# Products with v for two units at a time, a planner with other TensorE times, and the gather's place before the weight splits

## The chip, the cores and the metric

The kernel runs on one core of a Trainium2 chip. The metric is the time of one execution on the device in microseconds (us). A core has five engines with an instruction queue each: TensorE (PE, with PEld for its weight loads), VectorE (DVE), ScalarE (ACT), GpSimd (POOL) and SyncE (SP, which here only issues DMAs). An engine takes its instructions in the order in which they stand in its queue; engines wait for each other through semaphores.

## The reference, cut to what matters

```python
def _attn_ref(q, k, v):                      # 4 x 8 x 576 x 64
    scores = scale * np.matmul(q, k.transpose(0, 1, 3, 2))
    kth = np.partition(scores, -32, axis=-1)[..., -32:-31]
    scores = np.where(scores >= kth, scores, -1000000000.0)
    attn = np.exp(scores - np.max(scores, axis=-1, keepdims=True))
    attn = attn / (np.sum(attn, axis=-1, keepdims=True) + 1e-09)
    return np.matmul(attn, v)
def _moe_ref(x, w_in, w_out):                # 2304 x 512 x 2048
    h = x @ w_in
    return (h * np.cos(h)) @ w_out
def _moe2_ref(x, w_gate, w1, w2):            # 8 experts, 288 tokens each
    order = np.argsort(-(x @ w_gate).flatten())
    for idx in order:                        # a token goes to its best expert that has room
        ...
    for e in range(8):
        out[assigned == e] = np.maximum(x[assigned == e] @ w1[e], 0.0) @ w2[e]
    return out
```

## The kernel before, in words

**Attention.** The rows of the score matrices are handled in 72 units: 8 for the last 64 rows of the heads (called remainder units), then 64 that each hold 128 rows of two heads. For a unit, PE makes the scores (`qk`, L592), ACT takes them out of PSUM (L599), DVE finds the 32nd largest of each row with rounds of MAX8 and MATCH_REPLACE (L633 to L649), ACT and POOL mask and exponentiate (L664 to L676), DVE zeroes what lies below the threshold and sums (`zero`, L681). Then PE transposes the weights (L745 to L749), ACT copies them out (`eT`, L755), and PE multiplies them with v (`pv`, L770 and L772; L777 and L779 in remainder units). Beside that runs the divisor: POOL makes it from the sums (`div`, L797), DVE inverts it (`recip`, L794), POOL widens it (`wide`, L800), PE transposes it (`Rm`, L805), ACT copies it out (`R`, L809), and DVE scales the product into `xr` (`scale`, L823; L820 in remainder units). Before, each of these steps is made once per unit.

**MLP.** Every 8 units fill a block of 256 tokens (9 blocks). A block's `xr` is split into a high and a low part (L873, L878), multiplied with w_in in three products (`mm1`, L328, 12 matmuls a step), passed through h*cos(h) (L340 to L369 on ACT, DVE and POOL), split again (L893, L897) and multiplied with w_out (`mm2`, L912). Its rows of y go to DRAM, and its gate logits are made on PE (L935 to L965).

**Tail.** When the attention is over, constants are set on POOL and DVE (`late_consts`, L1068 to L1102, the last of them `wog_`, the gate weights that the logits of the last block need). The last block's MLP, its logits (`lg4`, L396) and the routing in rounds (`cmp` L1194, `cnt` L1200) follow, beside the last block's y. The routing ends in `idx` (L1378). POOL then gathers the first expert's rows with indirect DMAs (`xg`, L1417), while DVE makes the low parts of the first experts' weights (`w2l`, task `wlo`, L1048). Then the loop over experts runs: gather (L1563), transposes (L1627, L1631), first product (L1584), `hl` (L1588), second product (L1599). It splits weights `LA` chunks ahead.

**What sets the order.** Class `Plan` is a list scheduler that runs when the program is built. Each step is a task with an engine, a duration in ns, the tasks that it follows, the buffers that it takes and gives, and a rank to which a number from the tables `OFFSETS` and `TAIL_OFFSETS` is added. At each step the planner starts the task that can start first; among those of one engine that are within a small margin the lower rank wins. It adds `SW` = 95 ns when PE changes its tiling (table `MODE`: 64x128 for `qk`, 128x64 for `pv`, 128x128 for most others). The result is only an order of instructions on each engine: on the chip an instruction waits for the semaphores of its own operands and buffers and for nothing else that the planner thought of.

Of the kernel before, what the change touches and what calls it, by code (L numbers as in the profile page):

```python
# [9 lines left out]
F32 = mybir.dt.float32  # L10
# [13 lines left out]
NCAND = 8  # L24


def f32(ap):
# [11 lines left out]
    "L": -3.75, "Re": -2.25, "Re_0": -5.5, "Re_r": 6, "Rm": 4, "Rm_0": -2.25, "Rm_r": 5.5, "bias": 7, "bias_0":  # L39
    -4.75, "bias_r": 6.5, "big": 5.75, "big_0": 5.75, "big_r": -0.5, "count": 3.25, "div": -7.75, "div_0": 1.75,  # L40
    "div_r": 5, "eT": -2.25, "eT_0": -8.25, "eT_r": 2.75, "evac": -4.25, "evac_0": -7.25, "evac_r": -3.5, "exp":
# [3 lines left out]
    "less_0": -1.25, "low_in": -5.75, "low_out": -3, "mag_in": 2.5, "mag_out": 8, "mask": 2.75, "mask_0": 3,  # L45
    "mask_r": -3, "mm1": 3.75, "mm1_0": 5.5, "mm2": 9.25, "mm2_0": 10, "near": 0, "near_0": -4.75, "other": 2,
    "other_0": -1.5, "other_r": 4, "pl": 2.25, "pv": 0.75, "pv_0": -9.5, "pv_r": -4.25, "qk": -0.5, "qk_0": -4.5,
    "qk_r": 4.25, "recip": -1.25, "recip_0": 6, "recip_r": -2.5, "scale": 3.25, "scale_0": -8.75, "scale_r": 4.25,
    "sg_in": -2.75, "sg_out": 2.25, "shift_in": -10, "shift_out": 3, "sine": -4, "sine_0": 5, "small": 5, "small_0":
    -4.25, "small_r": -7.25, "strike": 5.75, "strike_0": 8, "strike_r": 10, "top": 8, "top_0": 10, "top_r": -4.75,  # L50
    "total": -8.75, "tr": 3.25, "tr_0": -4, "tr_r": 7.75, "v": 3.75, "wH_in": 3, "wH_out": -1.25, "wL_in": -10,
    "wL_out": -6.5, "w_in": 7, "w_out": 10, "whole": -0.5, "wide": 8, "wide_0": 7.25, "wl": 4.25, "wl_0": -5, "wp":
    1, "wraw_in": 3.25, "wraw_out": 8.75, "wse": 2, "wst_out": -4.75, "wt": -9.75, "wte": -5, "xH": -9.75, "xL":
    -0.5, "yT": 2.5, "yd": -1.75, "ys": 2.5, "yt": 4.5, "zero": -7.5, "zero_0": 4, "zero_r": -8.25
# [5 lines left out]
    "L": 7, "all": 2.25, "am": -7, "amd": 5.25, "any": 4.5, "asg": -8.75, "before": 1.25, "cmp": 1.5, "cnt": -2.75,  # L60
    "columns": 5.75, "excess": -8, "first": -7, "gH": -8.25, "gH_e": 2.25, "gL": 3, "gL_e": -8.5, "gate": 7.25,
    "go": 1.25, "here": 2.5, "higher": 4.75, "hot": -0.5, "hs": -7.25, "in_column": -3.25, "in_row": -2.5, "less":
    1.75, "lg": 3.5, "lg4": 3.25, "listed": -3.25, "lt": 9.25, "mm1": -5, "mmT": -1.75, "near": 0, "next": 0,
    "numbers": 9, "places": 0.25, "prop": 4.5, "rise": 7.75, "rows": 2.25, "shares": 4.25, "sine": 2.75, "slots": 3,
    "square": 3.5, "start": 2, "sums": -4.25, "tokens": -1, "verdict": 2, "wh": 3.25, "wl": 4, "wlo": 6.25, "woL":
    4.25, "woL_e": 3.5, "woL_f": 4.5, "wrong": -3.25, "xg": 7.5, "y": 1, "y_e": 0.75, "y_f": -4.75, "yd": 3.5,
    "yd_e": -3, "yd_f": 3, "ys": 7, "ys_e": 9.75, "ys_f": 0.5, "z": 3.25, "zd": -2.75
# [3 lines left out]
class Plan:  # L71
# [6 lines left out]
    SW = 95  # L78
    HOLD_PE = 0
# [9 lines left out]
    def add(self, key, eng, ns, fn, after=(), take=(), give=(), rank=0, table=None, lat=0):  # L89
# [4 lines left out]
        port = eng == "POOL" and key[0] != "xg" or eng == "DVE" and key[0] in self.PORT and not (key[0] == "less" and key[1] in LESS_DVE)  # L94
# [40 lines left out]
    def run(self):  # L135
# [29 lines left out]
        while len(order) < len(ts):  # L165
# [27 lines left out]
            if t["mode"]:  # L193
                f = work(s, t["ns"] + (self.SW if t["mode"] != mode else 0))
                mode = t["mode"]
            else:
                f = s + t["ns"] + (self.TABLE if sw else 0)
# [23 lines left out]
def fused_kernel(ctx: ExitStack, tc: tile.TileContext, qT: bass.AP, kT: bass.AP, qR: bass.AP, kR: bass.AP, v9: bass.AP,  # L221
# [62 lines left out]
    def everything(fold, ctx):  # L284
# [30 lines left out]
        def hidden1(plan, T, psum, mp, m, need, rank, stay=None):  # L315
# [103 lines left out]
        def phase1():  # L419
# [13 lines left out]
            for vt in vts:  # L433
# [6 lines left out]
                kp=3, qp=2, vt=2, x=3, m8=3, nm=2, w=2, tb=2, eT=4, rs=2, ri=2, rw=1, R=2, xr=1, xHL=1,  # L440
                hs=3, kr=1, gH=2, gL=2, wl=4, ys=2, yT=1)
# [134 lines left out]
            def qk(j):  # L576
# [27 lines left out]
                for c in range(2):  # L604
                    last = [("qk", j, 0)] if c else [("qk", j - 1, 1)] if j else []
                    add(("qk", j, c), "PE", 1160 if rem else 590, prod(c), need + last, [("pS", j, c)], give, rank=j - 1)
# [3 lines left out]
            def topk(j):  # L610
# [60 lines left out]

                def expo(h):
                    if ("rs", j) not in T:
                        new(ap, "rs", j, [128, 2])
                    sums = T["rs", j][:, h:h + 1]
                    A.activation(w_(h) if mode == "T" else x_(h), x_(h), AF.Exp, bias=T["nm", j][:, h:h + 1], scale=0.125,  # L676
                                 accum_out=None if mode == "T" else sums)

                def zero(h):
                    sums = T["rs", j][:, h:h + 1]  # L680
# [34 lines left out]
                for h in range(2):  # L715
# [5 lines left out]
                    rs = [("rs", j)] if h == 0 else []  # L721
# [6 lines left out]

            def pv(j):

                rem, b, hp, t = unit(j)
                u = key(j, 0)

                parts = [(h, n) for h in range(2) for n in range(5)] if rem else [(None, n) for n in range(9)]
                chunks = [parts[a:a + 3] for a in range(0, len(parts), 3)]
# [22 lines left out]
                def prod():  # L758
                    o_ = new(psum, "pT", ("pv", j), [128, 128])
                    if rem:  # L760
                        o_ = o_.rearrange("p (h q) -> p h q", h=2)
                    for c, i in [(c, i) for c in range(len(chunks)) for i in range(len(chunks[c]))]:
                        h, n = chunks[c][i]
                        eT = T["eT", (j, c)][:, i, :]
                        for a in range(2):
                            p = slice(a * 64, (a + 1) * 64)
                            if h is None:
                                o = o_[p]
                                if n == 8:
                                    PE.matmul(o, T["vt", u][:, 8 + a], eT, start=False, stop=True)  # L770
                                elif n % 2 == a:
                                    PE.matmul(o, T["vt", u][:, n, :], eT, start=(n < 2), stop=False)  # L772
                            else:
                                o = o_[p, h]
                                v = T["vt", u + h]
                                if n < 4:
# [933 lines left out]
```

## Time and profile before

| | us |
|---|---|
| median of 3 runs (1118.85, 1121.01, 1121.40) | 1121.01 |
| the profiled execution, time | 1117.51 |
| the profiled execution, span from first to last instruction | 1115.5 |
| PE busy | 1031.5 (92%) |
| DVE busy | 915.9 (82%) |
| ACT busy | 799.6 (72%) |
| POOL busy | 546.9 (49%) |
| mean granted TensorE clock | 0.966 |

An engine's busy share is an average over stages: the attention with the MLP of the earlier blocks, the tail, and the experts. The stages are read apart below. The granted clock is a share of TensorE's full speed of 2.4 GHz; 0.50 is its lower level, 1.2 GHz, and numbers between are mixtures of the two in one stretch.

### The profile page before, as it was taken

To read this page: it belongs to the slowest core of one execution; us is meant where nothing else is said; L and a number is where in the kernel's file an instruction comes from. 1 tells how busy PE (TensorE), PEld (TensorE's weight loads), DVE (VectorE), ACT (ScalarE), POOL (GpSimd) and SP (SyncE) were. 2 spreads that over 40 slices of the span, in tenths; PEclk is the share of its full clock that TensorE was granted. 3 is DMA by queue.
4 is the path that set the end of the run, shared out by engine and by line. 5 is a ranking of instruction groups with operands and counts; after the bars stand their busy time and mean duration, and the time that the engine had idled before them with its cause. 6 is when DMAs were issued, how large, how long until landed. Compare 5 with 4: busy or idle time off the path is not lost. (4 is left out here: it accounts for less than half of the span.)

```text
span 1115.5 us, 22521 instructions
## 1 busy us (share of the span) xinstructions
PE 1031.5 (92%) x7972; PEld 866.0 (78%) x7972; DVE 915.9 (82%) x2510; ACT 799.6 (72%) x1463; POOL 546.9 (49%) x710
## 2 busy tenths in 40 slices
PE   4666998899999999999999999998998899999995
PEld 1444876677888878878888888887866799999995
DVE  6999999999999999999999999995497455555530
ACT  4887889798988988888888988987420455555531
POOL 5985777766655654654755655655002202222211
PEclk9987898999999999999999999999999799999998
DMA  7474533434423323333233233212258746666601
GB/s 234 153 223 155 169 110 106 158 112 127 123 90 102 94 84 109 99 85 110 82 94 117 85 93 108 86 50 67 78 168 286 249 152 194 194 195 195 195 26 39
DMA packets 88441, 144.97 MB, mean 130 GB/s; under 512 B 15744, under 2 KB 36736, under 8 KB 88320
## 3 DMA queue, kind: packets, MB, share of 16 engines
q1 hardware_dynamic: 85248, 134.01, 38.6%
q0 software_dynamic: 3072, 9.44, 3.0%
q8 instruction: 65, 1.06, 0.4%
q14 instruction: 56, 0.46, 0.1%
HBM read 129.52 MB, written 13.89 MB: 129 GB/s over the span
## 5 line engine op out<-in xcount | busy, mean ns | idle before, releaser
L642 DVE MAX8 m<-w 128x8 f32<-128x288 f32 (+1 forms) x576 | 239.1, 449 | 1.5
L646 DVE MATCH_REPLACE8 w<-m,w 128x288 f32<-128x288 f32 x432 | 189.0, 442 | 0.0
L328 PE MATMUL pH<-xH,wiH 128*128 128x256 f32 x576 | 174.8, 304 | 3.8 <-DVE kr L359 3.3
L328 PE MATMUL pH<-xL,wiH 128*128 128x256 f32 x576 | 164.1, 285 | 0.0
L328 PE MATMUL pH<-xH,wiL 128*128 128x256 f32 x576 | 164.0, 285 | 0.0
L592 PE MATMUL two<-kp,qp 64*128 64x288 f32 (+1 forms) x640 | 129.0, 491 | 28.8 <-ACT x L599 18.8
L670 POOL TENSOR_TENSOR x<-x,w 128x576 f32<-128x576 f32 x76 | 109.5, 1455 | 29.2 <-ACT w L664 29.0
L755 ACT ACTIVATE eT<-pT 128x384 f32<-128x384 f32 x224 | 105.7, 479 | 24.2 <-PE pT L745 18.6
L328 PEld LDWEIGHTS pH<-xH,wiH 128*128 128x128 f32 x576 | 111.3, 193 | 8.6 <-DVE kr L359 4.4
L1048 DVE TENSOR_TENSOR w2l<-w2raw,w2h 128x1024 fp32r<-128x1024 f32 x64 | 77.9, 1224 | 41.2 <-ACT w2h L1045 39.2
L328 PEld LDWEIGHTS pH<-xL,wiH 128*128 128x128 f32 x576 | 111.3, 193 | 0.3
L328 PEld LDWEIGHTS pH<-xH,wiL 128*128 128x128 f32 x576 | 111.0, 193 | 0.0
L1616 POOL DMA_INDIRECT out<-ot,idx x24 | 22.3, 930 | 178.7 <-ACT ot L1614 178.3
L599 ACT ACTIVATE x<-two 128x576 f32<-128x576 f32 x144 | 93.5, 649 | 19.4 <-PE two L592 10.8
L592 PEld LDWEIGHTS two<-kp,qp 64*128 64x128 f32 (+1 forms) x640 | 49.6, 188 | 68.5 <-ACT x L599 28.9
L745 PE MATMUL pT<-ident,x 128*128 128x128 f32 x576 | 97.7, 279 | 3.3 <-DVE x L681 1.2
L369 POOL TENSOR_TENSOR hs<-hs,kr 128x512 f32<-128x512 f32 x56 | 75.6, 1368 | 42.9 <-ACT kr L364 41.8
L912 PE MATMUL pY<-wo,gH 128*128 128x512 f32 x224 | 96.4, 430 | 0.0
L745 PEld LDWEIGHTS pT<-ident,x 128*128 128x128 f32 x576 | 67.8, 142 | 30.0 <-issue 14.0
L897 POOL TENSOR_TENSOR gL<-hs,gH 128x512 fp32r<-128x512 f32 x56 | 75.8, 1353 | 30.8 <-ACT gH L893 24.7
L912 PE MATMUL pY<-wl,gH 128*128 128x512 f32 x224 | 88.2, 394 | 0.0
L912 PE MATMUL pY<-wo,gL 128*128 128x512 f32 x224 | 87.9, 392 | 0.0
(228 smaller groups left out, 2939.8 us busy)
## 6 DMA issues: line engine op xcount, KB each, us to landing
w2raw<-w SPq DMA_DIRECT2D x64, 512.0 KB, 4.7
wl<-wl_d SPq DMA_DIRECT2D x112, 256.0 KB, 2.7
vt<-v SPq DMA_DIRECT2D x48, 256.0 KB, 2.7
woL<-wl_d SPq DMA_DIRECT2D x46, 256.0 KB, 3.8
kp<-kT SPq DMA_DIRECT2D x32, 288.0 KB, 3.1
room<-w_in SPq DMA_DIRECT2D x16, 512.0 KB, 4.3
room<-w_out SPq DMA_DIRECT2D x16, 512.0 KB, 3.5
kp<-kR SPq DMA_DIRECT2D x16, 288.0 KB, 4.5
```

The costliest lines, as they stand in the source:

```text
L328: PE.matmul(ph, lw[:, c, fs], rx[:, c, :], start=(k == 0), stop=(k == 3 * KD - 1))
L369: (G if m - 1 + i in GATE_POOL else V).tensor_tensor(h, h, T["kr", m // 2][:, 2 * i:2 * i + 2], op=OP.mult)
L592: PE.matmul(o, lhsT, T["kp", us[h]][p, s], start=True, stop=True)
L599: A.activation(T["x", j][:, :, c * hS:(c + 1) * hS], T["pS", (j, c)][:, :, :hS], AF.Copy)
L642: V.max(m8_(h, 8 * k), w_(h, 0, hS + (8 if k == TOPK // 8 - 1 else 0)) if fold else w_(h))
L646: V.match_replace(w, m8_(h, 8 * k), x_(h) if k == 0 and not fold else w, -BIG)
L670: G.tensor_tensor(x_(h), x_(h), w_(h), op=OP.subtract if mode == "S" else OP.add)
L745: PE.transpose(pT[:, i, :], e[:, c0:c0 + 128], ident)
L755: A.activation(new(ap, "eT", (j, c), [128, 3, 128])[:, :n], T["pT", ("e", j, c)][:, :n], AF.Copy)
L897: (G if m in GL_POOL else V).tensor_tensor(gL, T["hs", m], f32(T["gH", m]), op=OP.subtract)
L912: PE.matmul(T["pY", blk][t], T[g, m][:, i, ts], w, start=(f == 0 and n == 0), stop=(f == KF - 1 and n == 2))
L1048: eng.tensor_tensor(WS[n][1], WR.pop(n), f32(WS[n][0]), op=OP.subtract)
```

## The change

Four things change. The steps from `div` to `scale` are made once for two units (a group) in every unit that is not a remainder; the number of matmuls is the same, the other instructions become half as many and twice as wide. The planner gets other durations for PE's tasks, a price for each change of tiling from a table, a margin in rank (`HOLD_PE` = 8) against changing it, and new tables of offsets, so that the order changes on every engine. Buffers change: `eT` 4 to 7, `R` 2 to 1, `ys` 2 to 1 in the attention, `kr` 1 to 2 in the tail, and some tiles of the routing share memory. The low parts of the weights are planned behind the third gather, and `LA` goes from 9 to 6. The numbers of the two tables tell nothing and are left out.

```diff
-    "L": -3.75, "Re": -2.25, "Re_0": -5.5, "Re_r": 6, "Rm": 4, "Rm_0": -2.25, "Rm_r": 5.5, "bias": 7, "bias_0":
+    "L": 4.5, "Re": 0.75, "Re_0": 10, "Re_r": -4.25, "Rm": 0.25, "Rm_0": -4.5, "Rm_r": 4.75, "bias": 4.5, "bias_0":
...
-    SW = 95
-    HOLD_PE = 0
+    SWITCH = {("128x128", "64x128"): 92, ("64x128", "128x128"): 229, ("64x128", "128x64"): 228, ("128x128", "128x64"): 131,
+              ("128x64", "128x128"): 414, ("128x64", "64x128"): 414}
+    def switch(self, old, to):
+        return 0 if to in (None, old) else self.SWITCH.get((old, to), 150)
+    HOLD_PE = 8
...
-        port = eng == "POOL" and key[0] != "xg" or eng == "DVE" and key[0] in self.PORT and not (key[0] == "less" and key[1] in LESS_DVE)
+        port = eng == "POOL" or eng == "DVE" and key[0] in self.PORT and not (key[0] == "less" and key[1] in LESS_DVE)
...
-                add(("mm1", m, i), "PE", 1440, one(i), after, [] if i else [("pH", m)], [("xHL", m // BW)], rank=rank)
+                add(("mm1", m, i), "PE", 1508, one(i), after, [] if i else [("pH", m)], [("xHL", m // BW)], rank=rank)
...
-                kp=3, qp=2, vt=2, x=3, m8=3, nm=2, w=2, tb=2, eT=4, rs=2, ri=2, rw=1, R=2, xr=1, xHL=1,
-                hs=3, kr=1, gH=2, gL=2, wl=4, ys=2, yT=1)
+                kp=3, qp=2, vt=2, x=3, m8=3, nm=2, w=2, tb=2, eT=7, rs=2, ri=2, rw=1, R=1, xr=1, xHL=1,
+                hs=3, kr=1, gH=2, gL=2, wl=4, ys=1, yT=1)
...
+            def group(j):
+                return j if j < NWR else NWR + (j - NWR) // 2
+            def members(g):
+                return [g] if g < NWR else [2 * g - NWR, 2 * g - NWR + 1]
+            def together(g):
+                js = members(g)
...
+                    o_ = new(psum, "pT", ("pv", g), [128, 128 * len(js)])
...
-                add(("pv", j), "PE", 1700 if rem else 985, prod, need + [("Rm", j)] + ([("pv", j - 1)] if j else []), [("pT", "pv", j)],
+                add(("pv", g), "PE", 1700 if rem else 1658, prod, eTs + [("v", u)] + ([("v", u + 1)] if rem else []) + [("Rm", g)] + ([("pv", g - 1)] if g else []),
...
-                        V.tensor_mul(xr[:, hp, t % 2 * 128:(t % 2 + 1) * 128], o_, R[:, 0])
+                        V.tensor_mul(xr[:, hp], o_, R.rearrange("p i q -> p (i q)"))
...
-        NCH, LA, NRAW = 12, 9, 4
+        NCH, LA, NRAW = 12, 6, 4
...
-        plan.bufs.update(pH=2, pY=2, pt=1, pc=1, pp=1, xHL=1, kr=1, gH=7, gL=7, woL=6, ys=1, lg=1, w2raw=NRAW)
+        plan.bufs.update(pH=2, pY=2, pt=1, pc=1, pp=1, xHL=1, kr=2, gH=7, gL=7, woL=6, ys=1, lg=1, w2raw=NRAW)
...
-                add(("wlo", n), "DVE", 1200, lambda: w_low(n, V), [("wh", n), ("tokens", )], give=[("w2raw", n)], rank=rank)
+                add(("wlo", n), "DVE", 1200, lambda: w_low(n, V), [("wh", n), ("xg", 2) if fold else ("tokens", )], give=[("w2raw", n)], rank=rank)
```

The line numbers after the change are higher by 5 (MLP) to 37 (the end of the attention's units), and by 35 in the tail.

**TensorE in the steady part of the attention.** Before, one unit's product with v (L772 and L770, 20 matmuls in 10 rows of order) stands between two stretches of MLP or scores:

```order
L328 MATMUL pH<-xL,wiH 128x256
L328 MATMUL pH<-xH,wiL 128x256
L592 MATMUL two<-kp,qp 128x288 x2
L772 MATMUL pT<-eT,vt_123 64x128 x8
L770 MATMUL pT<-eT,vt_123 64x128 x2
L745 MATMUL pT<-ident,x 128x128 x3
L912 MATMUL pY<-wo,gH 128x512
```

Now the products of two units stand together (L810 and L808), and the stretches between them are twice as far apart:

```order
L333 MATMUL pH<-xL,wiH 128x256
L333 MATMUL pH<-xH,wiL 128x256
L597 MATMUL two<-kp,qp 128x288 x2
L810 MATMUL pT<-eT,vt_122 64x128 x8
L808 MATMUL pT<-eT,vt_122 64x128 x2
L810 MATMUL pT<-eT,vt_122 64x128 x8
L808 MATMUL pT<-eT,vt_122 64x128 x2
L597 MATMUL two<-kp,qp 128x288 x2
```

What moved: every second entry into the tiling of the products with v, and every second way out of it, is gone.

**TensorE at the end of the attention.** Before, the last products with v are followed by 96 rows of the last block's `mm1` (L328), and only then by the logits that need `wog_` (L396):

```order
L745 MATMUL pT<-ident,x 128x128 x9
L805 MATMUL pT<-ident,rw 128x128
L772 MATMUL pT<-eT,vt_123 64x128 x8
L770 MATMUL pT<-eT,vt_123 64x128 x2
L328 MATMUL pH<-xH,wiH 128x256
L328 MATMUL pH<-xL,wiH 128x256
...
L328 MATMUL pH<-xH,wiL 128x256
L396 MATMUL pp<-room,wog__10014 32x256 x16
L328 MATMUL pH<-xH,wiH 128x256
```

Now the rows of y and of the gate (L980, L992) and the 16 matmuls of `lg4` that need `wog_` (L401) stand ahead of every `mm1` of the last block (L333):

```order
L810 MATMUL pT<-eT,vt_123 64x128 x8
L808 MATMUL pT<-eT,vt_123 64x128 x2
L810 MATMUL pT<-eT,vt_123 64x128 x8
L808 MATMUL pT<-eT,vt_123 64x128 x2
L980 MATMUL pT<-ident,ys 128x128 x4
L992 MATMUL pT<-wg,yT 128x8 x4
L401 MATMUL pp<-room,wog__9662 32x256 x16
L333 MATMUL pH<-xH,wiH 128x256
L333 MATMUL pH<-xL,wiH 128x256
```

What moved: `lg4` of the block before the last went from behind 96 rows of `mm1` to ahead of all of them.

**DVE at the gather and the first expert.** Before, the low parts of the weights (L1048) stand right behind `idx` (L1378), and three more of them stand between the parts of the first expert's rows (`xl`, L1567) and `hl` (L1588):

```order
L1378 TENSOR_SCALAR idx<-idf 96x24
L1048 TENSOR_TENSOR w2l<-w2raw,w2h 128x1024 x6
L1567 TENSOR_TENSOR xl<-po_11137,xh 128x288
L1567 TENSOR_TENSOR xl<-po_11138,xh 128x288
L1567 TENSOR_TENSOR xl<-po_11139,xh 128x288
L1567 TENSOR_TENSOR xl<-po_11140,xh 128x288
L1048 TENSOR_TENSOR w2l<-w2raw,w2h 128x1024 x3
L1588 SCALAR_TENSOR_TENSOR hl<-ph,hh 128x288
```

Now two small operations of the routing (`fl`, `fa`) stand between `idx` (L1413) and the low parts (L1082), and none stands ahead of the first `hl` (L1623):

```order
L1413 TENSOR_SCALAR idx<-idf 96x24
L1321 TENSOR_REDUCE fl<-c_9674 128x1
L1325 TENSOR_TENSOR fa<-fc,fl 128x1
L1082 TENSOR_TENSOR w2l<-w2raw,w2h 128x1024 x6
L1602 TENSOR_TENSOR xl<-po_10782,xh 128x288
L1602 TENSOR_TENSOR xl<-po_10783,xh 128x288
L1602 TENSOR_TENSOR xl<-po_10784,xh 128x288
L1602 TENSOR_TENSOR xl<-po_10785,xh 128x288
L1623 SCALAR_TENSOR_TENSOR hl<-ph,hh 128x288
L1082 TENSOR_TENSOR w2l<-w2raw,w2h 128x1024
```

What moved: three of the nine low parts that stood ahead of the first `hl` went behind it; the first six still follow `idx`, with no instruction between that waits for the gather.

## Rows read from the trace of the kernel before

**Rows 1.** Stages (us, busy us of PE, PEld, DVE, ACT, POOL, granted clock, DMA share).
```profile
50.00:100.00 50.00, 34.34 (x334) 21.52 (x332) 48.59 (x138) 39.82 (x81) 36.73 (x39) 0.80 0.65 201
...
400.00:450.00 50.00, 50.00 (x403) 40.31 (x398) 47.98 (x148) 41.72 (x76) 24.10 (x36) 1.00 0.34 100
...
900.00:950.00 50.00, 50.00 (x391) 50.00 (x390) 28.43 (x42) 26.58 (x45) 7.70 (x11) 1.00 0.57 176
```

**Rows 2.** Waits of PE, 0 to 300 (total, times, longest); two MAX8 in DVE's timeline.
```profile
PE two L592 <- ACT x L599: 18.8, 18, 3.3
...
407.16 0.82 DVE L642 MAX8 m<-w 128x8 f32<-128x288 f32 x2
```

**Rows 3.** Waits of PE and then of DVE, 300 to 765.
```profile
PE pT L805 <- POOL rw L800: 0.2, 1, 0.2
...
DVE xr L823 <- PE pT L770: 5.8, 18, 0.7
```

**Rows 4.** One product with v on PE (timeline); PE instructions (x) in two windows.
```profile
407.50 1.09 PE L772 MATMUL pT<-eT,vt 128*64 128x128 f32 x16
...
408.74 0.50 PE L912 MATMUL pY<-wo,gH 128*128 128x512 f32 x1
...
407.70:408.14 0.44, 0.44 (x12) 0.44 (x10) 0.44 (x3) 0.43 (x2) 0.44 (x1) 1.00 0.57 74
407.70:408.58 0.88, 0.88 (x20) 0.87 (x16) 0.88 (x5) 0.87 (x2) 0.88 (x2) 1.00 0.71 177
```

**Rows 5.** Groups by line on DVE and ACT (busy us, mean ns, idle before).
```profile
L823 DVE TENSOR_TENSOR xr<-pT,R 128x128 f32<-128x128 f32 x64 | 18.2, 284 | 10.9 <-PE pT L770 9.9 <-ACT x L676 0.5
...
L794 DVE RECIPROCAL ri<-ri 128x2 f32<-128x2 f32 x72 | 11.0, 152 | 4.3 <-POOL ri L797 3.8
...
L809 ACT ACTIVATE R<-pT 128x128 f32<-128x128 f32 x64 | 17.8, 278 | 0.3 <-PE pT L805 0.2
...
L809 ACT ACTIVATE R<-pT 128x256 f32<-128x256 f32 x8 | 3.0, 375 | 2.3 <-PE pT L805 2.3
```

**Rows 6.** End of the attention phase: DVE, PE, and a window of clock.
```profile
776.32 0.56 DVE L1102 COPY wog__10014<-wog 128x128 f32<-128x128 f32 x1
776.80 1.28 DVE L359 TENSOR_TENSOR kr<-pH,kr 128x512 f32<-128x512 f32 x2
...
768.57 0.28 PE L328 MATMUL pH<-xH,wiL 128*128 128x256 f32 x1
...
772.53 0.28 PE L328 MATMUL pH<-xH,wiL 128*128 128x256 f32 x1
...
777.50:780.00 2.50, 2.47 (x11) 2.47 (x12) 1.28 (x2) 1.15 (x1) 2.50 (x3) 0.50 0.64 221
```

**Rows 7.** The gather: timeline of DVE, POOL and PE.
```profile
854.98 0.17 DVE L1378 TENSOR_SCALAR idx<-idf 96x24 int32<-96x24 f32 x1
855.07 4.62 DVE L1048 TENSOR_TENSOR w2l<-w2raw,w2h 128x1024 fp32r<-128x1024 f32 x4
...
855.50 5.21 POOL L1417 DMA_INDIRECT xg<-y_d,idx  x1 [44.99 <-DVE idx L1378]
...
862.24 0.92 POOL L1417 DMA_INDIRECT xg<-y_d,idx  x1 [0.30 <-issue]
...
867.61 5.98 PE L1627 MATMUL po<-ident,xg 96*128 96x96 f32 x24 [6.43 <-DMA xg<-y_d,idx]
```

**Rows 8.** First expert: DVE, PE, and two windows after it.
```profile
878.42 3.50 DVE L1048 TENSOR_TENSOR w2l<-w2raw,w2h 128x1024 fp32r<-128x1024 f32 x3 [0.49 <-issue]
881.83 0.45 DVE L1588 SCALAR_TENSOR_TENSOR hl<-ph,hh 128x288 fp32r<-128x288 f32 x1
...
882.33 0.40 PE L1584 MATMUL ph<-xh,w2h 128*128 128x288 f32 x1 [2.17 <-DVE hl L1588]
...
882.50:885.00 2.50, 2.50 (x14) 2.50 (x15) 1.42 (x3) 1.11 (x2) 0.00 (x0) 0.63 1.02 296
885.00:887.50 2.50, 2.50 (x15) 2.50 (x15) 2.16 (x3) 1.42 (x2) 0.00 (x0) 0.68 1.07 374
```

More of the change, by code (lines that the diff above doesn't have):

```diff
@@ L47 @@
[L47 to L51, printed above, removed]
@@ new lines @@
+    -6.75, "low_out": -10, "mag_in": 7, "mag_out": -2.75, "mask": 0.25, "mask_0": -5, "mask_r": 0, "mm1": 3.5,
+    "mm1_0": 4.75, "mm2": 8.5, "mm2_0": 3.5, "near": 7.75, "near_0": 8.5, "other": 3.25, "other_0": 8.75, "other_r":
+    -0.25, "pl": 10, "pv": 2.5, "pv_0": -5.25, "pv_r": 5.25, "qk": -8.75, "qk_0": -2.25, "qk_r": -0.75, "recip":
+    -8.75, "recip_0": -7, "recip_r": -8, "scale": -4.75, "scale_0": -6.5, "scale_r": 0.5, "sg_in": -2.25, "sg_out":
+    -7.25, "shift_in": -3.5, "shift_out": -7.75, "sine": 10, "sine_0": 10, "small": -9.25, "small_0": -4.75,
@@ L59 @@
 TAIL_OFFSETS = {
[L60 to L67, printed above, removed]
+    "L": -5.75, "all": -5, "am": 8.75, "amd": -3.5, "any": 6.5, "asg": -3.25, "before": -2.5, "cmp": 8, "cnt": 7,
+    "columns": 7.25, "excess": 5, "first": 5, "gH": 7.25, "gH_e": 8, "gL": -2.5, "gL_e": -1.25, "gate": 1.25, "go":
+    -2.25, "here": 5.5, "higher": 5, "hot": -5.25, "hs": -4.5, "in_column": -6.75, "in_row": 7, "less": 4.5, "lg":
+    -10, "lg4": 5.75, "listed": 4, "lt": -7.75, "mm1": 7.25, "mmT": 3.5, "near": 4.25, "next": 0, "numbers": 0.5,
+    "places": 5.5, "prop": -5.75, "rise": 9, "rows": -9.5, "shares": -7.5, "sine": 2.25, "slots": -3.75, "square":
+    1, "start": -5.25, "sums": 7, "tokens": -2.75, "verdict": 5.25, "wh": -0.75, "wl": 2.5, "wlo": -3, "woL": -4.25,
+    "woL_e": -4.25, "woL_f": 1.25, "wrong": 2.25, "xg": 2.75, "y": -8.75, "y_e": 1.25, "y_f": -1.25, "yd": -5.5,
+    "yd_e": -7.75, "yd_f": -1.5, "ys": 6, "ys_e": -2, "ys_f": 4.75, "z": -3.5, "zd": 4.5
 }
@@ L193, in run @@
             if t["mode"]:
-                f = work(s, t["ns"] + (self.SW if t["mode"] != mode else 0))
+                f = work(s, t["ns"] + self.switch(mode, t["mode"]))
                 mode = t["mode"]
@@ L727, in topk, with parts_of @@
                         add(("zero", i), "DVE", 740, lambda h=h: zero(h), [("exp", i)], give=w + m8, rank=j + 1)
+            def parts_of(j):
+                parts = [(h, n) for h in range(2) for n in range(5)] if j < NWR else [(None, n) for n in range(9)]
+                return [parts[a:a + 3] for a in range(0, len(parts), 3)]
             def pv(j):
[L731 to L735, printed above, removed]
+                rem = j < NWR
+                chunks = parts_of(j)
                 rank = j + 1
@@ L756, in out_ @@
                     return fn
[L758 to L776, printed above, removed]
-                                    PE.matmul(o, v[:, 2 * n + a, :], eT[:, p], start=(n == 0), stop=False)
-                                else:
-                                    PE.matmul(o, v[:, 8 + a, :], eT[:, p], start=False, stop=True)
                 for c in range(len(chunks)):
@@ L783, in pv @@
                     last = [("tr", j, c - 1)] if c else [k for k in [("tr", j - 1, 3), ("tr", j - 1, 2)] if k in plan.tasks][:1]
-                    if j and c == (0 if rem else 1):
-                        last.append(("pv", j - 1))
-                    add(("tr", j, c), "PE", 15 + 108 * n, turn(c), [("zero" if MODES[j] == "T" else "exp", 2 * j + h) for h in range(2)] + last, [("pT", "e", j, c)],
+                    if j and c == (0 if rem else 1) and (("pv", group(j) - 1) in plan.tasks):
+                        last.append(("pv", group(j) - 1))
@@ L881, in block @@
                 for c in range(HP):
-                    need = [("scale", w) for w in last if unit(w)[2] // 2 == c // 2] if blk == 0 else [("scale", last[2 * c + i]) for i in range(2)]
+                    need = [("scale", w) for w in last if unit(w)[2] // 2 == c // 2] if blk == 0 else [("scale", group(last[2 * c]))]
                     add(("xH", blk, c), *(("DVE", 340) if (blk, c) == LAST else ("ACT", 310)), x_high(c), need + ([("xH", blk, c - 1)] if c else []),
@@ L1166, in all_max @@
             return r
-        av = small("av", [128, NTI, E])
-        vv = small("vv", [128, NTI, E])
+        avv = small("avv", [128, 2, NTI, E])
+        av, vv = avv[:, 0], avv[:, 1]
         best = small("best", [128, NTI])
```

123 lines of the change are left out of this document (78 added, 45 removed), and 7 rows, old and new, of the table OFFSETS.

## The prediction

> **What bounds the kernel now.** I read the busy times by stage first, then the waits of the engine that is not full, then the timeline at the places where the order changes. Early in the attention DVE is the full engine: between 50 and 100 us it is busy for 48.59 of 50 us and PE for 34.34 [rows 1], and PE's largest wait up to 300 us is for score tiles that ACT has to empty, 18.8 us in 18 pieces [rows 2]; ACT in turn waits for units that DVE has not finished. From some 300 us to the end of the attention at about 768 us PE is full (50.00 of 50 us at 400) with DVE close behind at 47.98 [rows 1]. In that stretch PE's waits are of 0.2 us, while DVE waits 5.8 us for products with v [rows 3]. So DVE's work counts for the first 300 us and PE's own work for the next 470. Then come the tail, with waits on every engine, and the experts, where PE is full at clock 1.00 and DVE at 28.43 of 50 us [rows 1].
>
> **The two-unit products, on PE.** One product with v holds PE from 407.50 to 408.74 us, 1.24 us for 20 matmuls [rows 4]. Inside it, widening a window by 0.44 us adds 8 matmuls (12 to 20), so one takes 0.055 us and twenty 1.10 [rows 4]. The other 0.14 us is the way into and out of the tiling. The two-unit form makes this once for two units. By the order, 48 of the 64 units are scaled in the stretch where PE is full, so 24 visits go there: 24 x 0.14 = −3.4 us. In the DVE-bound stretch a shorter PE gives nothing. The bounds are nothing (the entry is hidden by the weight load) and 24 x 0.28 = −6.7 (both neighbours of a visit also become cheaper); I take the value of the row. The planner's new table instead prices the way out at 0.414 us, which would be 24 x 0.414 = −9.9; a visit that costs 1.24 in all with 1.10 of matmuls leaves no room for that. The Trainium skill ("TensorEngine Tiling (Array Packing)", Key Properties) says that a change of tiling mode drains TensorE; the rows agree and give the drain its size, 0.14 us, and by the planner's reading of that rule the term would be the −9.9.
>
> At the end of the attention the last pair is one visit instead of a visit that was partly made earlier: its second 1.10 us now lies behind the last unit's transposes, which is the path. That is +1.1.
>
> **The two-unit divisor and scaling, on DVE.** A scaling takes 284 ns and an inversion 152 [rows 5]. What doubling the width costs DVE is not in the trace; ACT's copy of the same size goes from 278 to 375 ns when its width doubles, 97 ns for 128 more columns [rows 5]. I take a wide scaling at 0.42 us, some 0.15 less than two, and an inversion saved at 0.10, since neighbours overlap: 0.25 us for a pair. Bounds are 0 and 0.44 (284 + 152, the whole second pair of operations). Ahead of the scaling of the 16th unit that is 8 x 0.25 = −2.0 (0 to −3.5). By the order four operations of the top-32 that stood ahead of this point now stand behind it, and one `kr` more stands ahead: net −1.5 at 0.5 us each, an estimate between a MAX8 (two in 0.82 us [rows 2]) and a `kr` (two in 1.28 [rows 6]). Together −3.5 for the DVE-bound stretch. In the PE-bound stretch the 24 x 0.25 = 6 us saved on DVE are worth nothing; they lengthen DVE's waits for products. POOL and ACT, at 24.10 and 41.72 of 50 us in that stretch [rows 1], are not what PE waits for, so half as many `wide` and `R` go at nothing. `R` and `ys` with one buffer each hold the next `Rm` or y row until DVE or the DMA is done; with PE's waits in this stretch at 0.2 us [rows 3] I take nothing, at most +2.
>
> Sum to the end of the attention: −3.4 + 1.1 − 3.5 = **−5.8** (−10 to +2).
>
> **The end of the attention.** DVE sets the tail's constants and ends them with `wog_`, which runs from 776.32 to 776.88; from 776.80 it makes `kr` of the last block [rows 6]. Before, PE uses this time: 33 `mm1` matmuls take 3.96 us (768.57 to 772.53), 0.12 each, and 48 of them, as many as PSUM holds, end at 774. Now `lg4` waits for `wog_` at the head of PE's queue, 8.3 us after the 768.57, and all `mm1` of the last block queue behind it. The DVE instructions of this chain and their order are the same, so the chain is as late as before. So 48 x 0.12 = 5.8 us of products that were hidden come behind it, and the first `kr` on DVE has to wait for the first 24 of them. What the last block loses is 5.8, plus some of the low clock: already after a pause of 3 us PE ran at 0.50 between 777.5 and 780 [rows 6], and now it pauses for 8. Against it stand two `kr` buffers in place of one, which free DVE of waits for ACT's sine. Sum **+6.2** (+4 to +8). The rounds behind it keep their form: I find +1.4 and −1.3 from single small operations that change places, and take nothing.
>
> **The gather.** Before, DVE's four low parts run from 855.07 to 859.69 without a gap and the first gather instruction on POOL takes 5.21 us from 855.50; the third, alone, takes 0.92 [rows 7]. PE then waits 6.43 us for the gathered rows, until 867.61 [rows 7]. This is the loss that the new order of `wlo` aims at: 4.3 us. But the planner's dependency puts no wait on DVE. The low parts follow `idx` after two small operations, about 0.3 us later, still before POOL's 855.50, so that four of them again run ahead of and through the gather: **0**, against −4.3 if the gather gets in first. The Trainium skill ("SBUF — State Buffer", SBUF: two separate sides) has a shared port that a GpSimd operation or a DVE operation with two SBUF inputs holds for a whole instruction. By the letter of it POOL would come in after the first low part; the row shows it kept out through four.
>
> **The first expert.** Three low parts (3.50 us from 878.42) stand ahead of `hl` at 881.83, PE idles 2.17 us for it, and then runs 5 us at clock 0.63 and 0.68 [rows 8]. At full clock these 5 us would be 3.3. Without the three low parts `hl` comes at once: −2.2, and −1.7 for the clock if the pause was what lowered it. I take **−3.6** (−1 to −4). The three parts are made a few us later in a stage where DVE has over 20 of 50 us free [rows 1], so their move costs nothing unless the first chunk that they make is used within those us.
>
> **Sum.** −5.8 + 6.2 + 0 − 3.6 = −3.2. The profiled execution took 1117.51 us, which is 3.5 under the median of 1121.01, so against the median the time is 1121.01 − 3.2 = **1117.8 us**, against the profiled execution 1114.3.
>
> **Rivals.** *First block late.* By the order, seven MAX8, six MATCH_REPLACE and one conversion of weights (L481) more stand on DVE ahead of the scaling of the last remainder unit, which is most of one more unit's top-32. At 0.41 us a piece (two MAX8 in 0.82 [rows 2]) that is 14 x 0.41 = 5.7 us more DVE work ahead of the first block's `mm1`, in a stretch where DVE has 1.4 us of slack in 50 [rows 1]. If PE, which fills up only after 300 us, does not catch this up, the −3.5 becomes +2.2; with the +6.2 at the end of the attention at +8 and the −3.6 at −2, the sum is −3.4 + 1.1 + 2.2 + 8 − 2 = +5.9, 1126.9. It decides if block 1's first product starts later than now. Against it: that extra unit is work done ahead, so DVE has less behind it. *The gather gets ahead.* If the two small operations take longer than POOL's 0.35 us from `idx` to gather, POOL is first and the gather takes 0.92: −3.2 − 4.3 = −7.5, 1113.5. *DVE was the bound throughout.* PE in its full stretch may only look full because its operations stretch while waiting; then the attention ends earlier by all 32 x 0.25 = 8 us of DVE and 1.5 of moved operations: −9.5 + 1.1 + 6.2 − 3.6 = −5.8, 1115.2; DVE's 5.8 us of waits for PE speak against it [rows 3]. *The switch is dear.* With 0.414 for each the −3.4 is −9.9 and the sum −9.7, 1111.3; the 1.24 us visit speaks against it.
>
> **How the numbers follow.** About 0.3% or 3.4 us is what a measurement of this kernel can tell from no change. My forecast, −3.2, lies on that edge: chance 0.55, somewhat under half of it faster by more than that, the rest the same. First block late, 0.18, nearly all slower. Gather ahead 0.12, DVE the bound 0.08, the dear switch 0.07, all faster. So faster 0.21 + 0.27 = 0.48, same 0.34, slower 0.18. The range leaves out the ends of the dear switch and half of the late block: 1109 to 1125.
>
> **What would show it.** Right: visits of 2.3 us for two units; 8 us of PE idle ahead of `lg4` at the end of the attention, and the attention itself 6 us shorter; the first gather instruction again at 4 to 5 us; no wait of 2 us for the first `hl`. Wrong: an attention that ends later than 768 us, a tail from there to `idx` that is not longer than now, or a gather of 0.9 us.

## The result, and the profile after

The changed kernel took 1107.07 us in the median of four runs, against 1120.19 us for the kernel before on the same chip: ratio 0.9892, interval 0.9864 to 0.9920. Measured once more, in four runs, it took 1106.79 us against 1120.27: 0.9870 (0.9852 to 0.9888). So it is faster by 13 us, where 3.2 were forecast, and the time lies 2 us below the range.

| | before | after |
|---|---|---|
| profiled execution, us | 1117.51 | 1107.21 |
| its span, us | 1115.5 | 1105.4 |
| PE busy, us | 1031.5 | 1029.3 |
| DVE busy, us | 915.9 | 911.2 |
| last scaling of the attention starts at | 767.9 | 760.5 |
| last `mm1` of the last block starts at | 798.4 | 798.2 |
| `idx` starts at | 855.0 | 852.8 |
| first product of the experts starts at | 876.6 | 867.8 |

The two profiled executions differ by 10.1 us of span. Along the table: the attention ends 7.4 us earlier, all of it is given back at its end (+7.2), the rounds to `idx` win 2.0, the stretch from `idx` to the first expert's first product wins 6.7, and the experts behind it 1.2.

**Visits and wide operations.** The timeline of PE after shows one visit for two units. Compare it with [rows 4], where one visit for one unit lasts 1.24 us.

```profile
411.80 1.09 PE L810 MATMUL pT<-eT,vt 128*64 128x128 f32 x16
412.72 0.39 PE L808 MATMUL pT<-eT,vt 128*64 128x128 f32 x4
412.94 1.04 PE L810 MATMUL pT<-eT,vt 128*64 128x128 f32 x16
413.81 0.39 PE L808 MATMUL pT<-eT,vt 128*64 128x128 f32 x4
414.13 0.76 PE L597 MATMUL two<-kp,qp 64*128 64x288 f32 x4
```

It lasts from 411.80 to 414.13, 2.33 us, where two visits of before take 2.48: 0.15 us saved, as forecast. The groups of DVE after, by line, answer to [rows 5]:

```profile
L855 DVE TENSOR_TENSOR xr<-pT,R 128x256 f32<-128x256 f32 x32 | 13.6, 424 | 9.6 <-PE pT L808 9.4
...
L826 DVE RECIPROCAL ri<-ri 128x4 f32<-128x4 f32 x32 | 5.3, 167 | 0.3 <-POOL ri L829 0.3
```

A wide scaling takes 424 ns, an inversion of four columns 167 ns.

**The end of the attention.** Timeline of PE, then of DVE, then a window of the clock, all after; they answer to [rows 6].

```profile
760.06 0.39 PE L808 MATMUL pT<-eT,vt 128*64 128x128 f32 x4
...
761.98 1.06 PE L992 MATMUL pT<-wg,yT 128*128 128x8 f32 x8 [0.94 <-ACT yT L985]
769.62 3.64 PE L401 MATMUL pp<-room,wog__9662 128*32 128x256 f32 x32 [6.59 <-POOL gL L1483]
...
768.85 0.56 DVE L1137 COPY wog__9662<-wog 128x128 f32<-128x128 f32 x1
...
765.00:767.50 2.50, 0.00 (x0) 0.00 (x0) 2.34 (x3) 1.10 (x3) 2.44 (x4) 0.50 0.48 166
```

PE stands idle for 6.59 us and goes on at 769.62, 0.2 us after the end of `wog_`. (The profile names `gL` on POOL as what ended the wait, but these 16 matmuls need `wog_`, which DVE finished at 769.41.) The granted clock in the idle stretch is 0.50, and it is still 0.50 from 770 to 772.5 us, so that `lg4` takes 3.64 us for 32 records.

**The gather and the first expert.** Timelines of DVE, POOL, PE and SP's queue after, which answer to [rows 7, 8]:

```profile
852.81 0.17 DVE L1413 TENSOR_SCALAR idx<-idf 96x24 int32<-96x24 f32 x1
...
853.16 4.62 DVE L1082 TENSOR_TENSOR w2l<-w2raw,w2h 128x1024 fp32r<-128x1024 f32 x4
...
853.29 2.10 POOL L1452 DMA_INDIRECT xg<-y_d,idx  x1 [45.19 <-DVE fa L1325]
...
860.39 2.92 PE L1662 MATMUL po<-ident,xg 96*128 96x96 f32 x24 [0.69 <-ACT y L1497]
...
867.76 0.40 PE L1619 MATMUL ph<-xh,w2h 128*128 128x288 f32 x1 [2.48 <-ACT xh L1601]
...
860.80 0.32 SPq L1501 DMA_DIRECT2D y_d<-y  x1
861.18 13.77 SPq L1074 DMA_DIRECT2D w2raw<-w  x7
```

The same queue before, in its timeline:

```profile
857.21 1.74 SPq L1040 DMA_DIRECT2D w2raw<-w  x3
869.12 0.34 SPq L1466 DMA_DIRECT2D y_d<-y  x1
869.55 1.60 SPq L1040 DMA_DIRECT2D w2raw<-w  x3
```

The first gather instruction takes 2.10 us in place of 5.21, PE no longer waits for the rows at all (0.69 us, for ACT), and the 24 transposes take 2.92 us, at clock 1.00, in place of 5.98 at 0.50. On SP's queue, which the prediction did not read, three raw loads of 512 KB (weights before they are split) used to go out at 857.21, while the gather was under way. Now the store of the last y rows stands ahead of them and holds them back until 861.18, when PE is already transposing the rows.

### The profile page after: what moved, and what is told of

Same layout as the page of the kernel before. It is cut to its first block, busy times and chain, and to the rows that moved or that the text cites. A ratio compares the mean times of both kernels' runs of the same rounds, so it can differ in the third digit from the quotient of the medians.

```text
span 1105.4 us, 22341 instructions
## 1 busy us (share of the span) xinstructions
PE 1029.3 (93%) x7972; PEld 865.6 (78%) x7972; DVE 911.2 (82%) x2446; ACT 794.8 (72%) x1431; POOL 537.0 (49%) x646
## 4 chain that ended last, share of the span: by engine, by line
PE 50%; issue 19%; DVE 17%; POOL 8%; ACT 4%; DMA 1%; SPq 0%; POOLq 0%; DVEq 0%; ACTq 0%
PE pH L333 15%; PE pY L944 12%; PE two L597 7%; PE pT L757 5%; PE pT L810 4%; DVE m L647 3%; DVE w L651 2%; POOL out L1651 2%; POOL xg L1598 2%; DVE w L644 2%; DVE oa L1230 1%; DVE w L638 1%; DVE room L485 1%; POOL room L488 1%; PE pY L1490 1%
## 5 line engine op out<-in xcount | busy, mean ns | idle before, releaser
L333 PE MATMUL pH<-xH,wiH 128*128 128x256 f32 x576 | 172.7, 300 | 0.0
L333 PE MATMUL pH<-xL,wiH 128*128 128x256 f32 x576 | 162.6, 282 | 0.0
L333 PE MATMUL pH<-xH,wiL 128*128 128x256 f32 x576 | 162.6, 282 | 0.0
L597 PE MATMUL two<-kp,qp 64*128 64x288 f32 (+1 forms) x640 | 133.0, 505 | 21.7 <-ACT x L604 14.0
L333 PEld LDWEIGHTS pH<-xH,wiH 128*128 128x128 f32 x576 | 109.4, 190 | 11.6 <-issue 9.7
L1082 DVE TENSOR_TENSOR w2l<-w2raw,w2h 128x1024 fp32r<-128x1024 f32 x64 | 78.1, 1224 | 44.4 <-ACT w2h L1079 43.9
L333 PEld LDWEIGHTS pH<-xL,wiH 128*128 128x128 f32 x576 | 109.8, 191 | 0.7
L333 PEld LDWEIGHTS pH<-xH,wiL 128*128 128x128 f32 x576 | 109.5, 190 | 0.0
```

Of the source, the lines that this page charges most:

```text
L333: PE.matmul(ph, lw[:, c, fs], rx[:, c, :], start=(k == 0), stop=(k == 3 * KD - 1))
L597: PE.matmul(o, lhsT, T["kp", us[h]][p, s], start=True, stop=True)
L1082: eng.tensor_tensor(WS[n][1], WR.pop(n), f32(WS[n][0]), op=OP.subtract)
```

## The experiments

Ratios are to the kernel before on the same chip. Medians of different experiments can come from different chips; the kernel before had medians of 1119.9 to 1120.5 us on them. The texts set off are what was expected ahead of each run.

**The two halves apart.** The first kernel has the changed attention and plans the tail as before, with the `TAIL_OFFSETS` of before too; the diff is against the changed kernel. The second has it the other way round.

```diff
-        NCH, LA, NRAW = 12, 6, 4
+        NCH, LA, NRAW = 12, 9, 4
...
-        plan.bufs.update(pH=2, pY=2, pt=1, pc=1, pp=1, xHL=1, kr=2, gH=7, gL=7, woL=6, ys=1, lg=1, w2raw=NRAW)
+        plan.HOLD_PE, plan.switch = 0, lambda old, to: 0 if to in (None, old) else 95
+        plan.bufs.update(pH=2, pY=2, pt=1, pc=1, pp=1, xHL=1, kr=1, gH=7, gL=7, woL=6, ys=1, lg=1, w2raw=NRAW)
...
-                add(("wlo", n), "DVE", 1200, lambda: w_low(n, V), [("wh", n), ("xg", 2) if fold else ("tokens", )], give=[("w2raw", n)], rank=rank)
+                add(("wlo", n), "DVE", 1200, lambda: w_low(n, V), [("wh", n), ("tokens", )], give=[("w2raw", n)], rank=rank)
```

> The attention as changed, the tail in the order of before (its offsets, one kr buffer, the low parts behind the tokens, splits 9 ahead). Theory A, the sum of places read from the two profiles: the attention gives 7.4 us and nothing is lost at its end, since mm1 of the last block stands ahead of lg4 again, so 7.4 us under before (ratio 0.993). Theory B, all of the gain is the attention's and the tail gives nothing: 10 to 13 us under before (0.989). Theory C, the attention gives only what TensorE's visits save: 3.4 us (0.997).

> The attention of before, the tail as changed. Theory A: +7.2 at the end of the attention, 2.0 less in the rounds, 6.6 less at the gather and behind it, 1.3 less in the first expert, together 2.7 us under before (0.998). Theory B: no difference (1.000). The sum of the prediction for these places: +6.2 - 3.6 = 2.6 us over before (1.002).

Measured: 1112.77 us, ratio 0.9938 (0.9919 to 0.9957) for the new attention with the old tail, 1118.76 us, 0.9984 (0.9970 to 0.9998) for the other. Both are as theory A has them, and the second excludes the prediction's sum for the tail, 2.6 us over before. Their product, 0.9922, is 8.7 us; the whole change gives more, 0.9870 when it was measured again:

> The changed kernel once more, for a narrower interval. The two halves measured apart (0.9938 and 0.9984) give 0.9922 if they add up, 8.7 us; the first measurement, four runs, gave 0.9892.

So 3 to 6 us, by the first or the second measurement, seem to come only when both halves are there; the intervals of the three ratios together leave some 3 us of doubt. What makes this part is not shown.

**The gather alone.** Three kernels change the gather's place in the kernel before. In the first DVE really waits for the third gather, and the change's line on the low parts is in it too:

```diff
+            if i == 2 and fold:
+                G.memset(issued, 0.0)        # on POOL, behind the third gather
...
+                V.tensor_copy(seen, issued)  # on DVE, ahead of the first low part
...
-                add(("wlo", n), "DVE", 1200, lambda: w_low(n, V), [("wh", n), ("tokens", )], give=[("w2raw", n)], rank=rank)
+                add(("wlo", n), "DVE", 1200, lambda: w_low(n, V), [("wh", n), ("xg", 2) if fold else ("tokens", )], give=[("w2raw", n)], rank=rank)
```

> Before, with one thing added: DVE's first low part waits for a cell that POOL writes behind the third gather, so that the gathers run alone. Theory A (the gather is kept out by DVE, and the long pause of TensorE lowers its clock as well): the gathers take 0.92 us each, the transposes of the gathered rows start 4 to 5 us earlier and run at clock 1.00 in place of 0.50, 6 to 9 us under before less what the low parts, 3 us later, cost the first expert: 5 to 7 us under (0.995). Theory D (the gather alone): 4.3 us under (0.996). Theory E (the low parts are then late and take it back): within 1.5 us of before.

Measured: 1123.04 us, 1.0022 (1.0010 to 1.0034), slower. All theories fall on the time; theory E has the mechanism, but too small. The gathers ran alone (1.15, 0.92 and 0.92 us), and the first expert's first product came 17.7 us after `idx` in place of 21.6. Behind it all was lost again; the timeline of DVE and PE shows where:

```profile
864.51 0.14 DVE L1054 COPY seen<-issued 1x1 f32<-1x1 f32 x1 [4.02 <-POOL issued L1427]
...
874.88 1.22 DVE L1055 TENSOR_TENSOR w2l<-w2raw,w2h 128x1024 fp32r<-128x1024 f32 x1 [5.70 <-ACT w2h L1045]
...
888.12 0.61 PE L1593 MATMUL ph<-xh,w2h 128*128 128x288 f32 x1 [5.45 <-DVE hl L1597]
```

The low parts are 4 us late, so are the raw loads that take over their buffers, the high parts made from them, and the next low parts; with three of these ahead of `hl`, PE waits 5.45 us for it.

The second and third kernel put two and five small copies ahead of the low parts, where the change has `fl` and `fa`:

```diff
+                for i, t in enumerate(spare):         # two, or five
+                    V.tensor_copy(t, spare[i - 1] if i else cf[:, 0:1])
```

> Before, with two copies of one column (the second reads the first) on DVE between idx and the low parts, as the change has fl and fa there. Theory G, the place in time decides: the first low part starts some 0.3 us later, POOL's first gather then takes about 2.1 us in place of 5.2, TensorE reaches the first expert 4 to 5 us earlier, and the time falls by 3 to 5 us (ratio 0.996 to 0.997). Theory H, the small operations are not the reason (the prediction's view): the gather stays at 4 to 5 us and the time within 0.5 us of before.

> The same with five copies, so that the first low part starts some 0.9 us after where it started. Theory G: the first gather gets most of its work done ahead of it and takes 0.9 to 2.1 us, the gain is that of two copies, less what the low parts are late (under 1 us). Theory I, any delay of the low parts is paid in full by the loads that wait for their buffers, as with the true wait: the gain shrinks by 0.6 us against two copies or more. Theory H: as before.

Measured: 1121.54 us, 1.0000 (0.9987 to 1.0012), and 1120.83 us, 1.0003 (0.9991 to 1.0015). Theory G is right on the gather and wrong on the time; theory H is right on the time alone, and for another reason than its own. DVE, POOL, PE and SP's queue with two copies:

```profile
860.82 4.62 DVE L1055 TENSOR_TENSOR w2l<-w2raw,w2h 128x1024 fp32r<-128x1024 f32 x4
...
861.37 1.69 POOL L1424 DMA_INDIRECT xg<-y_d,idx  x1 [46.05 <-DMA woL<-wl_d]
...
862.69 2.01 SPq L1040 DMA_DIRECT2D w2raw<-w  x3
...
869.12 0.74 PE L1634 MATMUL po<-ident,xg 96*128 96x96 f32 x2 [0.69 <-ACT y L1469]
872.86 5.09 PE L1634 MATMUL po<-ident,xg 96*128 96x96 f32 x22 [2.99 <-DMA xg<-y_d,idx]
```

The gather is issued in 1.69 us, but most of its rows do not come sooner: after two transposes PE waits 2.99 us for the others and then runs 22 transposes at clock 0.50 (5.09 us). What the gather's instruction takes on POOL was not what PE waited for.

**The loads.** One line of the change undone in the changed kernel, and the same line alone in the kernel before:

```diff
-                add(("wlo", n), "DVE", 1200, lambda: w_low(n, V), [("wh", n), ("xg", 2) if fold else ("tokens", )], give=[("w2raw", n)], rank=rank)
+                add(("wlo", n), "DVE", 1200, lambda: w_low(n, V), [("wh", n), ("tokens", )], give=[("w2raw", n)], rank=rank)
```

In the changed kernel this moves nothing on DVE, PE, ACT and POOL; on SP's queue five raw loads stand ahead of the store of y again.

> The change with one line undone: the low parts planned behind the tokens again. The order on DVE, PE, ACT and POOL stays that of the change; on SP's queue alone the raw loads of the next weights stand ahead of the store of the last y rows again. Theory L, the loads are what the gathered rows wait for: the gathers are issued as in the change (2.1, 1.8, 0.9 us), but 1.5 MB of weights are moved at the same time, TensorE waits 3 to 6 us for the rows and falls to clock 0.50, and the time is 4 to 8 us over the change (1111 to 1115; 0.992 to 0.996 of before). Theory G, DVE's place alone makes the gain: the time of the change (1107; 0.988).

Measured: 1112.41 us, 0.9937 (0.9913 to 0.9960), 5.6 us over the changed kernel's second measurement by the medians (5 to 7.5 us by the ratios). Theory L holds. POOL, PE and SP's queue in its timeline:

```profile
852.55 2.11 POOL L1452 DMA_INDIRECT xg<-y_d,idx  x1 [45.19 <-DMA woL<-wl_d]
...
864.49 0.74 PE L1662 MATMUL po<-ident,xg 96*128 96x96 f32 x2 [3.29 <-DMA xg<-y_d,idx]
...
854.20 10.01 SPq L1074 DMA_DIRECT2D w2raw<-w  x5
865.61 0.34 SPq L1501 DMA_DIRECT2D y_d<-y  x1
```

The gather is issued exactly as in the change (2.11 us), the loads go out from 854.20, and the wait for the rows is back, 3.29 us, with clock 0.50 from 865 to 870 us behind it.

> Before with that one line of the change alone. On DVE, PE and POOL nothing moves, on SP's queue the store of the last y rows goes ahead of three raw loads. Theory L: the first gather is still kept out for 5 us by DVE, but its rows then come without the loads: TensorE's wait of 6.4 us becomes 3 to 4, 2 to 5 us under before if the loads, 4 us later, are not missed (0.996 to 0.998). Theory G: the time of before, since the gather is as late (1.000).

Measured: 1122.59 us, 1.0024 (1.0009 to 1.0038): slower. The line alone costs the kernel before 2.7 us. The first gather instruction is as long as before (5.03 us), and yet PE waits for the rows only 3.4 us in three pieces, the first of 1.83, as theory L has it. But the loads go out 10.8 us after `idx` in place of 2.2 and are missed, since three low parts stand ahead of `hl`, so the condition that theory L set for a gain does not hold:

```profile
867.70 0.43 PE L1627 MATMUL po<-ident,xg 96*128 96x96 f32 x2 [1.83 <-DMA xg<-y_d,idx]
...
888.27 0.61 PE L1584 MATMUL ph<-xh,w2h 128*128 128x288 f32 x1 [3.69 <-DVE hl L1588]
```

**Splits 6 ahead, alone.** In the kernel before:

```diff
-        NCH, LA, NRAW = 12, 9, 4
+        NCH, LA, NRAW = 12, 6, 4
```

> Before, with weights split 6 chunks ahead in place of 9, so that no low part stands ahead of the first hl. Theory A (read from the two profiles): 1.3 us under before. The prediction's term: 3.6 us under, 2.2 of the wait and 1.4 to 1.7 of the clock. Rival: the splits moved into the expert loop delay it, no difference.

Measured: 1115.78 us, 0.9965 (0.9951 to 0.9978), 3.9 us under before: the prediction's term holds, theory A and the rival fall. DVE goes from the rows straight to `hl`:

```profile
877.13 0.94 DVE L1567 TENSOR_TENSOR xl<-po,xh 128x288 fp32r<-128x288 f32 x2 [0.48 <-ACT xh L1566]
879.20 0.46 DVE L1588 SCALAR_TENSOR_TENSOR hl<-ph,hh 128x288 fp32r<-128x288 f32 x1 [1.12 <-ACT hh L1587]
```

**The three pieces together** in the kernel before: the line on the low parts, two small copies, and splits 6 ahead.

> Before with the three pieces at the gather and the first expert: the store ahead of the raw loads, two small copies ahead of the low parts, weights split 6 ahead. Attention and rounds as before. Theory L: from idx to the first expert's first product 15 to 17 us in place of 21.6, and none of it lost to late weights: 6 to 9 us under before (0.992 to 0.995). Theory N, the pieces add up as measured singly (0 for the copies, 3.9 for 6 ahead, that of the store): 4 to 6 us under.

Measured: 1113.97 us, 0.9957 (0.9940 to 0.9973), 4.8 us by the ratio, less than theory L's 6 to 9, though the first product comes 16.4 us after `idx`, as it has it. Singly they gave 0, −3.9 and +2.7, together −1.2. The difference of 3.6 us is just clear of the intervals of the four ratios, some 3.2 us together. The traces suggest why they need each other: with the splits behind `hl`, late loads are no longer missed, and with the loads held back, the early gather is worth something.

**The changed attention with the three pieces.** The changed attention, the tail in the order of before, and the three pieces:

> The attention as changed, with the order of before in the tail (mm1 of the last block ahead of lg4, so that TensorE is not idle for 8 us there) and the three pieces of the run before. If the places add up: 7 us of the attention and 6 to 9 of the pieces under before, 1104 to 1107, and with the new order's 2 us in the rounds missing. If the gather's gain also rests on the later end of the y products in the changed tail, 1108 to 1112.

Measured: 1101.94 us, 0.9853 (0.9825 to 0.9881), under both ranges expected. That is 5 us under the changed kernel by the medians, and its slowest run (1105.77) is under the fastest of the eight of the change (1106.52), though not all were on one chip; by the ratios it is only 2 us, with intervals that overlap, so how much it gains on the change is open. Against the kernel with the changed attention and the old tail alone (0.9938) the three pieces give 9.6 us here, where they gave 4.8 with the old attention: again some 5 us more with the changed attention, and here the tail keeps the order of before. `mm1` of the last block stands ahead of `lg4` again, and PE reaches the transposes with no wait for rows:

```profile
854.08 3.69 PE L1671 MATMUL po<-ident,xg 96*128 96x96 f32 x24 [0.69 <-ACT y L1506]
...
861.53 0.40 PE L1628 MATMUL ph<-xh,w2h 128*128 128x288 f32 x1 [0.90 <-ACT xh L1610]
```

The first expert starts at 861.5, 6.2 us before the changed kernel's 867.8.

**Pairs and order.** The pairs under the old planner, and single units under the new one. The cut shows the lines that matter; the first kernel also has the old tables and planner durations, the second also the buffers and durations that belong to single units:

```diff
+            plan.HOLD_PE, plan.switch = 0, lambda old, to: 0 if to in (None, old) else 95   # pairs, OFFSETS of before
...
-                return [g] if g < NWR else [2 * g - NWR, 2 * g - NWR + 1]                    # the other kernel
+                return [g]
```

> Before, with the steps for two units and their buffers alone: planner times, switch price and both tables of offsets as before, the tail as before. The prediction's terms: 3.4 us less on TensorE, 1.1 more at the end, 2.0 less on DVE at the start, together 4.3 us under before (0.996). Theory J, the gain of the attention (6.9 us, new attention with the old tail) is the pairs' and needs no new order: 6 to 8 us under. Theory K, it comes from the new order: within 1 us of before, or over it, since the offsets were made for other tasks.

> The change with the steps from div to scale once per unit again (and the buffers for that: four eT, two R), everything else as changed: planner, offsets, tail. Theory J, the pairs' own saving counts, 24 visits at 0.15 us on TensorE less 1.1 at the end, and 2 us on DVE at the start: 4 to 5 us over the change (1111 to 1112, 0.992 of before). Theory K, the order was found for pairs and only fits them: 10 us or more over the change, as the pairs were 14 us over before when planned by the old tables. Theory M, the order alone makes the gain of the attention: the time of the change, within 2 us.

Measured: 1134.54 us, 1.0117 (1.0100 to 1.0133), and 1138.97 us, 1.0158 (1.0134 to 1.0181). Both are far slower than either kernel. In both the last scaling starts at 788.4 us, 20 us later than before. In these two cases a table of offsets that was made for another set of tasks cost 13 and 18 us against the kernel before, so neither run prices the pairs or the order by itself. How the attention's gain divides between them stays open.

## Why the prediction was wrong, by its own steps

- **Products with v on PE, −3.4: right for the single visit.** A pair's visit saves 0.15 us (2.33 against 2 x 1.24), and the planner's 0.414 us for the way out was not found. What 24 of them make in the whole stretch is not measured alone.
- **Scaling and inversion on DVE: right in size.** A wide scaling takes 424 ns, 0.42 us was taken.
- **The attention, −5.8: the right direction, too small.** −7.4 between the two profiles, −9.9 when the spread of the kernel before is counted (next point). From the first `mm1` of the third block (304.5, before 306.4) to the last scaling it is 456.0 us, before 461.5: 5.5 less where PE is full, and the terms of the prediction for this stretch give only −3.4 + 1.1 = −2.3. The cut is not clean: 18 matmuls of `mm2` that ran inside this stretch now run ahead of it. So the term is mis-sized, and which part of it made the rest is not shown. The late first block, a rival, is there (its first `mm1` at 124.3 us, before at 117.1) and is made up by the third block: that rival falls.
- **The baseline.** The sum was made against a profiled execution 3.5 us under the median, and the difference was added as if it were the same for both kernels. It is not: the old attention has two kinds of start. The windows from 55 to 65 us of the profile of before, of the kernel with the true wait and of the change (busy us of PE, PEld, DVE, ACT and POOL, then the granted clock):

```profile
55.00:65.00 10.00, 7.61 (x83) 4.74 (x85) 9.92 (x30) 8.89 (x20) 7.47 (x10) 1.00 0.68 206
```

```profile
55.00:65.00 10.00, 9.23 (x69) 5.44 (x68) 8.07 (x28) 7.29 (x15) 5.15 (x8) 0.54 0.59 179
```

```profile
55.00:65.00 10.00, 6.96 (x65) 4.20 (x65) 8.88 (x28) 7.88 (x17) 8.69 (x9) 0.83 0.61 165
```

  In four of the eight profiles with the old attention the clock there is 1.00 and the last scaling starts at 767.3 to 769.1; in the other four it is 0.51 to 0.66 and the last scaling starts at 771.4 to 772.7. The five with the changed attention (clock 0.79 to 0.93) lie between 759.1 and 761.2, 760.1 in the mean. So against the mean of the old attention, 770.0, the gain is 9.9 us, not 7.4. The whole spread lies ahead of the third block: from there to the last scaling all eight take 461.4 to 461.6 us and all five 455.9 to 456.0.
- **The end of the attention, +6.2: right.** PE is idle for 6.59 us, 8 were forecast, and the last `mm1` gives back 7.2. From there to `idx` 2.0 are won, which I had at zero. DVE makes the bounds of the search (L1160 to L1181 of the changed kernel) from 775.7 to 779.8, between its waits for the last block. Before, it made them from 801.8 to 804.9, in between the last operations that the last logits need. Now these end 1.3 us earlier, and the rounds start 1.6 us earlier (`prop` at 805.27, before at 806.87).
- **The gather, 0: this step failed.** From `idx` to the first product 6.7 us are won. The prediction weighed only DVE and POOL, and even there was wrong: with two small operations ahead of the low parts POOL gets in after the first of them (2.10 us in place of 5.21). That is as the letter of the Trainium skill ("SBUF — State Buffer", SBUF: two separate sides) has it for POOL; the page also has the one that comes second blocked, and DVE was not, since its four low parts take 4.62 us in both kernels. But an earlier gather instruction alone is worth nothing, as two and five copies show (ratios 1.0000 and 1.0003), so the rival of −4.3 would have been wrong too. The gain is on SP's queue, where the change puts the store of y ahead of three raw loads; the prediction followed the moved low parts on DVE and not the loads that wait for their buffers. Undoing that costs 5.6 us.
- **The first expert, −3.6: right by itself, −3.9 measured alone.** In the change only 1.2 are seen behind the first product: PE idles 1.2 us right behind it and runs at 0.50 between 870 and 872.5 us. The later loads are part of the reason, since with them early again the stretch from the first product to the end is 1.7 us shorter (236.0 against 237.7).
- **The sum, place by place.** −9.9 + 7.2 − 2.0 − 6.7 − 1.2 = −12.6 us, close to the 13 measured, where the prediction has −5.8 + 6.2 + 0 + 0 − 3.6 = −3.2. So the gather taken at nothing is the largest miss (6.7), the attention with its baseline the second (4.1), the rounds the third (2.0); the other two places fell short by 3.4 together.

## What to carry to other kernels

When a step is moved or made to wait, follow the buffers that it frees: the loads queued behind them are moved as well, and what they then no longer collide with can be most of the gain. What a gather cost here was the time to the landing of its rows, not that of its instruction. And a sum made against one profiled execution holds only if both kernels scatter around their profiles alike; look at several profiles of the early, half-idle stretches first.

## What the runs showed of the hardware that was not expected

Where the low parts stand right behind `idx` on DVE, POOL's first gather instruction starts 0.43 to 1.28 us after the first low part and ends 5.6 us after that start, so it is kept out through all four; this is so in all five profiles of that kind, and the instruction takes 4.4 to 5.2 us. Where two small operations stand between `idx` and the low parts, it starts 0.13 to 0.55 us after the first low part and ends 2.2 us after that start, so it is kept out through one only; this is so in all eight profiles of that kind, and it takes 1.7 to 2.1 us. The moment of arrival does not decide it: a start 0.43 us after the first low part waited for four [rows 7], a start 0.55 us after it for one (861.37 against 860.82, with two copies). Why two small operations make the difference is not shown. The four low parts take 4.6 us either way, so DVE loses nothing when the gather gets in.

And the granted clock in a half-idle stretch differs between executions of one and the same attention (1.00 or 0.51 to 0.66 in the same 10 us). The old attention ends 4 us later where it is low. The five profiles of the new one end within 2.1 us of each other, but runs without a profile scatter by 5 us there as well (1109.5 to 1115.1 us with the old tail, 1106.5 to 1111.4 over the eight runs of the change), and where these arise no profile shows.
